# Row maxima in two groups per projection task of a transformer block, and more of them in pairs

## The chip, the cores and the metric

The kernel runs on one core of a Trainium2 chip. It uses that core's engines: TensorE (PE, with PEld for its weight loads), VectorE (DVE), ScalarE (ACT), GpSimd (POOL) and SyncE (SP), which here issues most of the DMAs. The metric is device time of one execution in microseconds (us), as the median of several runs. One further execution is profiled; its span, from the first to the last instruction, is the time base of every trace quoted here. The granted TensorE clock was 1.000 over the whole profiled span.

## The reference

One transformer block with adaptive layer norms, in fp32, on 2048 tokens of width 448:

```python
mod = (silu(c) @ w_mod).reshape(1, 6, 1, -1)      # sa, ca, ga, sb, cb, gb
h = layernorm(x) * (1 + ca) + sa
qkv = h @ wqkv                                     # 16 heads of 28
scores = einsum("bhqd,bhkd->bhqk", q, k) * 28**-0.5
o = einsum("bhqk,bhkd->bhqd", softmax(scores), v)
x = x + ga * (o @ wo)
h = layernorm(x) * (1 + cb) + sb
x = x + gb * (gelu(layernorm(h) @ w1 + b1) @ w2 + b2)   # w1: 448 x 1792
```

The weights are drawn large, so the scores are too, and the softmax needs the maximum of each row of scores before the exponentials.

## The kernel before

Tokens lie in four blocks of 512 and the 16 heads in four groups of four; a head is padded to 32 rows, so the four heads j of a group fill the 128 partitions in quarters. Most matrix products are made from two parts of each number (hi and lo in float32r), so a product over 448 has eleven terms: three row chunks with hi x hi, hi x lo and lo x hi, and two for the last half chunk.

**First phase** (0 to 181 us). After the first norm and the modulation, a loop over blocks b = 0 to 3 runs a list of tasks. A task is one product of eleven matmuls of 512 (or 448) columns into a PSUM tile `pa`: q or k of one head group (`qk_task`), or v of 128 tokens (`v_task`). Block 0 has 14 tasks, blocks 1 and 2 have 12, block 3 has 10, since q and k of head group 0 for the next block stand in the block before. In four tasks of blocks 0, 1 and 2 the next block's normalised tokens are transposed as well; I call them turning tasks.

**The row maxima.** The exact softmax maximum is not needed: the maximum of the hi parts' scores serves. For head group g, query block qt, key block cch, 128 queries i and head j, one matmul with 32 rows and 512 columns (`max_mm`, L392) writes 128 x 512 scores into a PSUM bank `mx` (or `o`), and VectorE reduces them to 128 numbers in `mxp` (`max_one`, L397). There are 4 x 4 x 4 x 16 = 1024 of these. For 48 places of head group 0, key blocks 0 and 1 are taken as a **pair**: one matmul with the difference of the two key tiles, a Relu on ScalarE into a third of `d0` (L405), one matmul with key block 0, and one VectorE operation that adds both and takes the maximum (L409). A pair has two matmuls, as two single maxima have, but one VectorE operation in place of two. When all 64 maxima of a head group and query block are there, `max_fin` reduces them over the key blocks (L429), and the result is written into spare rows of the stored q.

Behind each product of the first phase `emit_task` issues one group of maxima: the first matmuls of its pairs, two singles, the second matmuls of the same pairs, and the other singles. Block 0 has four VectorE operations per task, later blocks up to five; the last task of the phase has none. Five banks `mx`, one `o` and two `pa` are in use. The four quarters of the rows can hold four heads' matmuls side by side.

**Attention** (181 to 846 us). 16 units (head group, query block) of 16 steps. Step: twelve score matmuls in 32 rows (L1046) in two halves, two exponentials on ScalarE (L1051), four matmuls with v for the step before (L1016), and the maxima that the first phase left, in a fixed rhythm of 4 and 3 per step. `n_maxima` puts surplus ones into the steps of the last units that hold the output projection (steps 8 to 11 of units 12 to 15, L317); what is left after the last maximum runs without them. **MLP**: from 846 us on.

[...]

Of the kernel before, what the change touches and what calls it, by code (L numbers as in the profile page):

```python
# [22 lines left out]
D = 448  # L23
# [10 lines left out]
P1RATE = 4  # L34
# [7 lines left out]
def tile_adaln_block(ctx: ExitStack, tc: tile.TileContext, x, wqkv, wo, w1, b1, w2, b2, c, w_mod, out):  # L42
# [272 lines left out]
    def mm_acc(p, terms):  # L315
        for i, (a, b) in enumerate(terms):
            pe.matmul(p, a, b, start=(i == 0), stop=(i == len(terms) - 1))  # L317
# [18 lines left out]
    def qk_task(b, kind, g, done=0, begun=None):  # L336
        p, ts = begun or qk_terms(b, kind, g)
        for i in range(done, len(ts)):
            pe.matmul(p, *ts[i], start=(i == 0), stop=(i == len(ts) - 1))  # L339
# [12 lines left out]
        full = sbt("full", [128, 512], bufs=3)  # L352
        lo = sbt("lo", [128, 512], F32R, bufs=3)
        act.activation(full, p, AF.Identity, bias=bias)

        def split():
            (act.copy if b else dve.tensor_copy)(hi, full)
            if kind == 1 and (g, b) == (0, 1):
                k_diff.append(sbt("raw", [128, 512], F32R, bufs=3))
                pool.tensor_tensor(out=k_diff[0], in0=f(hi), in1=f(kh_sb[(0, 0)]), op=ALU.subtract)  # L360
            pool.tensor_tensor(out=lo, in0=full, in1=f(hi), op=ALU.subtract)
            sl = slice(b * 512, (b + 1) * 512)
            sp.dma_start(f(dscr[kind][0][g])[:, sl], f(hi))
            sp.dma_start(f(dscr[kind][1][g])[:, sl], f(lo))

        return split

    def v_task(b, t):
        p = ps_s()
        ts = slice(t * 128, (t + 1) * 128)  # L370
        hh, hl = hT[b]
        mm_acc(p[:, :D], terms448(
            lambda k: hh(k)[:, ts], lambda k: hl(k)[:, ts], lambda k: wv[0][:, k, :], lambda k: wv[1][:, k, :],
        ))
        emit_task(*p1_n)
        act.copy(v_sb[b][:, t, :, :DH], p[:, :D].rearrange("p (h d) -> p h d", d=DH))
# [6 lines left out]
    k_diff = []  # L383
    paired = ((0, 1), (0, 2), (0, 3))
# [16 lines left out]
    def pair_diff(g, qt, i, j):  # L401
        m = max_mm(g, qt, i, j, k_diff[0])
# [22 lines left out]
    def max_fin(g, qt):  # L425
        m32 = sbt("m32", [128, 32], F32R, bufs=2)
        c0 = 1 if (g, qt) in paired else 0
        pool.memset(f(m32)[:, 16:32], 0.0)
        dve.tensor_reduce(  # L429
            out=m32[:, 0:16].rearrange("p (h i) -> p h i", i=4),  # L430
            in_=mxp[(g, qt)][:, :, :, c0:].rearrange("p i h c -> p h i c"), op=ALU.max, axis=AX.X, negate=True,
        )
# [20 lines left out]
    def queue_max(g, qt, cch):  # L453
# [4 lines left out]
        if (g, qt) in paired and cch < 2:  # L458
            if cch == 1:
                pxq.extend((g, qt, i, j) for i in range(4) for j in range(4))  # L460
            return
        for i in range(4):
            for j in range(4):
                mxq.append((g, qt, cch, i, j))
# [38 lines left out]
    def emit_task(n, sixth, n_pairs):  # L503
# [3 lines left out]
        rests = [pair_diff(*m) for m in pairs]  # L507
        js = [m[3] for m in pairs]
        n_ops = n - len(pairs) + (sixth and len(pairs) > 0)
        singles = []  # L510
        for x in range(n_ops - len(pairs)):
            if mxq:

                free = [j for j in range(4) if j not in js] or range(4)
                fits = [y for y, m in enumerate(mxq[:16]) if m[:3] == mxq[0][:3] and m[4] == free[x % len(free)]]
                singles.append(mxq.pop(fits[0] if fits else 0))
        ops = [lambda ps, m=m: max_one(*m, ps) for m in singles]
        ops[2:2] = rests
        for x, op in enumerate(ops):
            op(ps_o if x + len(pairs) == 5 else ps_mx)  # L520
        for g, qt, cch, i, j in singles:
            count(g, qt, [cch])
        for g, qt, i, j in pairs:
            count(g, qt, [0, 1])

    p1_n = [0, False, 1]
# [25 lines left out]
    def mod_fin():  # L552
# [5 lines left out]
        for j, name in enumerate(("ga", "sb", "cb", "gb")):  # L558
# [41 lines left out]
    for b in range(NB):  # L600
# [11 lines left out]
        for n, (tb, kind, g) in enumerate(tasks):  # L612
            post = []
            ready, newq = newq, []
            p1_n[0] = P1RATE if b < 1 else P1RATE + 1
            if not more and n == len(tasks) - 1:
                p1_n[0] = 0

            k = n - (5 if b < 2 else 4)
            p1_n[1] = not (more and (0 <= k < NC)) and not (b == 1 and n < 4)  # L620
            p1_n[2] = (3 if n > 4 else 1) if b == 3 else 2 if b == 2 and p1_n[1] else 1
# [8 lines left out]
            else:  # L630
                v_task(tb, g)
            for item in ready:
                queue_max(*item)
# [43 lines left out]
    assert not pxq  # L677
# [23 lines left out]

    wo_p = [slot(f"e{part}", [128, NG, D]) for part in range(2)]
# [451 lines left out]
```

## Time and profile before

| | |
|---|---|
| median of 3 runs | 1149.93 us (1149.39 to 1150.04) |
| profiled execution: span | 1147.0 us |
| what the runs' median has beside that span | 2.93 us |
| TensorE busy | 1134.5 us (99%) |
| VectorE busy | 828.7 us (72%) |
| ScalarE busy | 682.5 us (60%) |
| GpSimd busy | 216.8 us (19%) |
| first score matmul of attention | 181.25 us |

A row of a timeline has the start in us, the duration of all its instructions together, engine, line, operation, tiles and shapes, their count, and in brackets the idle time ahead of it with what ended it. Matmuls are pipelined: their starts say how fast they follow each other, their ends are modelled. A row of groups has the busy sum and the mean duration in ns, then the engine's idle time ahead of these instructions. A row of waits has the engine and line that waited, what for, the sum in us, the number of times, and the longest.

### The profile page before, as it was taken

Reading aid. Unit: us, or ns where it says so; the run is one execution under the profiler, and the core shown is the slowest. Engines: PE = TensorE matmul, PEld = TensorE weight load, DVE = VectorE, ACT = ScalarE, POOL = GpSimd, SP = SyncE. Lnnn points to the kernel's source line nnn. Section 1 sums busy time; section 2 is a strip of 40 time slices with the busy share of each in tenths; the row PEclk is TensorE's granted clock in tenths of the full one; section 3 lists DMA queues with packets and bytes.
Section 4 is the critical chain, followed back from the end, with each engine's and each line's share of the span. In section 5 each row is a group of like instructions: output and inputs, shape, how many; then the busy total and the mean of one; then the engine's idle time right before and its main releaser. Section 6 shows DMA issues by size and latency. Waiting matters only on the chain.

```text
span 1147.0 us, 20808 instructions
## 1 busy us (share of the span) xinstructions
PE 1134.5 (99%) x8380; PEld 679.5 (59%) x8380; DVE 828.7 (72%) x1487; ACT 682.5 (60%) x839; POOL 216.8 (19%) x235
## 2 busy tenths in 40 slices
PE   8999999999999999999999999999999999999998
PEld 6767765444443444444444444545458888888887
DVE  6868788999998899989999977583648853444322
ACT  4656757777777877777877777675862321111110
POOL 2534432210000000000000011204514503123000
PEclk9999999999999999999999999999999999999999
DMA  9642354111132111321110222022213100000000
GB/s 299 204 148 110 107 184 130 44 60 57 45 96 66 57 39 38 94 66 57 59 55 21 83 84 62 24 84 68 68 46 95 42 33 1 1 33 1 33 1 33
DMA packets 51305, 81.09 MB, mean 71 GB/s; under 512 B 12700, under 2 KB 21760, under 8 KB 51208
## 3 DMA queue, kind: packets, MB, share of 16 engines
q1 hardware_dynamic: 50248, 78.73, 21.6%
q8 instruction: 66, 1.08, 0.4%
q0 software_dynamic: 672, 0.56, 0.2%
q10 hardware_dynamic: 288, 0.46, 0.1%
q14 instruction: 31, 0.25, 0.1%
HBM read 53.11 MB, written 26.35 MB: 69 GB/s over the span
## 4 chain that ended last, share of the span: by engine, by line
PE 96%; DVE 1%; ACT 1%; issue 1%; SPq 0%; DMA 0%; DVEq 0%; POOL 0%; POOLq 0%; ACTq 0%
PE s L1046 27%; PE o L1016 22%; PE mx L317 16%; PE pa L339 7%; PE mx L392 6%; PE s L1104 4%; PE s L1105 4%; PE s L1103 4%; PE pa L317 3%; PE pa L276 1%; PE o L240 1%; PE mx L240 1%; ACT slot_c L1051 0%; PE o L547 0%; PE pa L279 0%
## 5 line engine op out<-in xcount | busy, mean ns | idle before, releaser
L397 DVE TENSOR_REDUCE mxp<-mx 128x1 f32<-128x512 f32 x919 | 579.6, 685 | 105.9 <-PE mx L392 101.2
L1046 PE MATMUL s<-slot_b,slot_a 32*128 32x512 f32 x3072 | 383.7, 422 | 1.9 <-ACT full L814 0.7
L1051 ACT ACTIVATE slot_c<-s 128x1024 f32<-128x1024 f32 x342 | 331.6, 1022 | 83.8 <-PE s L1046 82.3
L1046 PEld LDWEIGHTS s<-slot_b,slot_a 32*128 32x128 f32 x3072 | 214.4, 183 | 254.5 <-ACT slot_c L1051 151.3
L392 PE MATMUL mx<-kh,qh 32*128 32x512 f32 x899 | 289.6, 470 | 1.2 <-DVE mxp L397 0.9
L1051 ACT ACTIVATE slot_d<-s 128x1024 f32<-128x1024 f32 x170 | 164.8, 1021 | 42.7 <-PE s L1046 42.6
L1016 PE MATMUL o<-slot_c,v 128*32 128x512 f32 x1368 | 183.1, 605 | 0.6 <-ACT osb L984 0.4
L1087 ACT ACTIVATE full<-mx,b_col 128x512 f32<-128x512 f32 x56 | 38.6, 689 | 191.8 <-PE mx L317 175.3
L392 PEld LDWEIGHTS mx<-kh,qh 32*128 32x128 f32 x899 | 116.1, 182 | 8.5 <-DVE mxp L397 5.2
L1090 DVE CAST hi<-full 128x512 fp32r<-128x512 f32 x56 | 25.2, 451 | 129.2 <-ACT full L1087 129.2
L783 POOL TENSOR_TENSOR osb<-osb,osb 128x512 f32<-128x512 f32 x16 | 20.9, 1305 | 463.4 <-DMA osb<-drec 295.1
L1016 PE MATMUL o<-slot_d,v 128*32 128x512 f32 x680 | 90.6, 605 | 0.0
L1016 PEld LDWEIGHTS o<-slot_c,v 128*32 128x32 f32 x1368 | 27.1, 108 | 57.5 <-issue 53.7
L317 PE MATMUL mx<-y,slot_a 128*128 128x512 f32 x160 | 60.6, 395 | 0.0
L405 ACT ACTIVATE slot_d<-mx 128x512 f32<-128x512 f32 x48 | 27.0, 596 | 40.1 <-PE mx L392 40.0
L1091 DVE TENSOR_TENSOR lo<-full,hi 128x512 fp32r<-128x512 f32 x56 | 44.1, 788 | 5.2
L317 PE MATMUL mx<-y,slot_c 128*128 128x512 f32 x152 | 47.5, 396 | 0.1
L1105 PE MATMUL s<-slot_v,lo 128*128 128x448 f32 x128 | 46.7, 365 | 0.0
L1103 PE MATMUL s<-slot_v,hi 128*128 128x448 f32 x128 | 46.6, 364 | 0.0
L317 PE MATMUL mx<-y,slot_v 128*128 128x512 f32 x112 | 39.2, 396 | 0.0
L317 PE MATMUL mx<-y,slot_b 128*128 128x512 f32 x112 | 39.1, 398 | 0.0
L339 PE MATMUL pa<-slot_c,slot_a 128*128 128x512 f32 x136 | 37.0, 405 | 0.0
(223 smaller groups left out, 1388.7 us busy)
## 6 DMA issues: line engine op xcount, KB each, us to landing
d<-lo SPq DMA_DIRECT2D x32, 256.0 KB
slot_b<-d SPq DMA_DIRECT2D x32, 256.0 KB
slot_a<-d SPq DMA_DIRECT2D x32, 256.0 KB
d<-hi SPq DMA_DIRECT2D x20, 256.0 KB
osb<-drec SPq DMA_DIRECT2D x14, 256.0 KB
out_dram<-xn SPq DMA_DIRECT2D x16, 224.0 KB
slot_v<-in_w_mod_dram SPq DMA_DIRECT2D x4, 784.0 KB
raw<-in_B_w_dram SPq DMA_DIRECT2D x14, 224.0 KB
```

Of the source, the lines that this page charges most:

```text
L317: pe.matmul(p, a, b, start=(i == 0), stop=(i == len(terms) - 1))
L339: pe.matmul(p, *ts[i], start=(i == 0), stop=(i == len(ts) - 1))
L392: pe.matmul(m, qh_sb[(g, qt)][js, i * 128 : (i + 1) * 128], k[js, :], start=True, stop=True)
L397: dve.tensor_reduce(out=mxp[(g, qt)][:, i, j, cch : cch + 1], in_=m, op=ALU.max, axis=AX.X)
L1016: pe.matmul(o[32 * j : 32 * j + 32, :], v_sb[kt // 4][:, kt % 4, 4 * g + j, :], p[:, j, :], start=(kt == 0), stop=(kt == NKT - 1),)
L1046: pe.matmul(s2[:, jj, :], ks[rows_, kp, kc], qs[rows_, qp, :], start=(term == 0), stop=(term == 2))
L1051: act.activation(pt[:, 2 * hf : 2 * hf + 2, :], s2, AF.Exp, scale=SCALE)
L1087: act.activation(gf, p, AF.Gelu_apprx_tanh, bias=b1_col[:, i : i + 1])
L1091: dve.tensor_tensor(out=glo, in0=gf, in1=f(ghi), op=ALU.subtract)
L1103: pe.matmul(pp, ghi[:, ts], w_hi, start=(m == 0), stop=False)
L1104: pe.matmul(pp, ghi[:, ts], w_lo, start=False, stop=False)
L1105: pe.matmul(pp, glo[:, ts], w_hi, start=False, stop=(m == NFT - 1))
```

## The change

1. **Two groups per task.** `mm_acc`, which issues a product's terms, can call a function ahead of its seventh term. From block 1 on `burst_mid` stands there: one single maximum and the second matmuls of the pairs begun behind the task before. Behind the product `burst_end` issues four maxima: the first matmuls of up to two pairs, and singles. A turning task begins one pair, others two; block 0 begins none before its last task.
2. **Which heads.** `pick` looks for heads that the group doesn't have yet.
3. **More pairs.** 56 places in place of 48: eight of head group 1, with a second difference tile (`make_diff`, made on GpSimd in block 1). `max_fin` reduces such a mixed query block in two pieces.
4. **Rows.** The second difference tile takes the place that held the broadcast rows sb and cb; these are now loaded when attention begins.

```diff
+    def mm_acc(p, terms, done=0, mid=None):
+        for i in range(done, len(terms)):
+            if i == 6 and mid:
+                mid()
+            pe.matmul(p, *terms[i], start=(i == 0), stop=(i == len(terms) - 1))
...
     def qk_task(b, kind, g, done=0, begun=None):
         p, ts = begun or qk_terms(b, kind, g)
-        for i in range(done, len(ts)):
-            pe.matmul(p, *ts[i], start=(i == 0), stop=(i == len(ts) - 1))
-        emit_task(*p1_n)
+        mm_acc(p, ts, done, burst_mid)
+        burst_end()
...
-    paired = ((0, 1), (0, 2), (0, 3))
+    paired = {(0, qt, i) for qt in range(1, 4) for i in range(4)} | {(1, 1, 0), (1, 1, 1)}
+
+    def make_diff(g, t):
+        k_diff[g] = t
+        pool.tensor_tensor(out=t, in0=f(kh_sb[(g, 1)]), in1=f(kh_sb[(g, 0)]), op=ALU.subtract)
...
-    def emit_task(n, sixth, n_pairs):
+    def pick(js):
+        for j in js:
+            fits = [y for y, m in enumerate(mxq[:16]) if m[:3] == mxq[0][:3] and m[4] == j]
+            if fits:
+                return mxq.pop(fits[0])
+        return mxq.pop(0)
+
+    rests = []
+
+    def singles(n, js, sixth):
+        picked = []
+        for _ in range(n):
+            if mxq:
+                picked.append(pick(js))
+                js = [j for j in js if j != picked[-1][4]]
+        for x, m in enumerate(picked):
+            max_one(*m, ps_o if sixth and x == n - 1 else ps_mx)
+        for g, qt, cch, i, j in picked:
+            count(g, qt, [cch])
+
+    def burst_end():
+        n, sixth, n_pairs, _ = p1_n
         if not n:
             return
         pairs = [pxq.pop(0) for _ in range(min(n_pairs, len(pxq)))]
...
+        rests.extend((m, pair_diff(*m)) for m in pairs)
+        used = [m[3] for m in pairs]
+        singles(n - len(pairs), [j for j in range(4) if j not in used], sixth)
+
+    def burst_mid():
+        now = rests[:]
+        rests.clear()
+        used = [m[3] for m, _ in now]
+        singles(p1_n[3], [j for j in range(4) if j not in used], False)
+        for m, rest in now:
+            rest(ps_mx)
+        for (g, qt, i, j), _ in now:
             count(g, qt, [0, 1])
...
-            p1_n[0] = P1RATE if b < 1 else P1RATE + 1
-            if not more and n == len(tasks) - 1:
-                p1_n[0] = 0
...
+            turning = more and 0 <= k < NC
+            last = not more and n == len(tasks) - 1
+            sixth = not turning and not (b == 1 and n < 4)
+            p1_n[:] = [0 if last else 4, sixth, 0 if b == 0 and n < 13 else 1 if turning else 2, 0 if b == 0 else 1]
```

What stands where now. On TensorE, between two products at the start of block 3, the order was this (`pa` is a product, `raw` the difference tile, `kh_69` key block 0, `kh_417` key block 3, `qh_407` query block 3, `qh_54` query block 0):

```order
L339 MATMUL pa_1805<-slot_c_355_1490,slot_a2h_128 128x512
L392 MATMUL mx_1818<-raw_725,qh_407_1718 128x512
L392 MATMUL mx_1821<-kh_417_1756,qh_54_329 128x512
L392 MATMUL mx_1824<-kh_417_1756,qh_54_329 128x512
L392 MATMUL mx_1827<-kh_69_382,qh_407_1718 128x512
L392 MATMUL mx_1830<-kh_417_1756,qh_54_329 128x512
L392 MATMUL o_1833<-kh_417_1756,qh_54_329 128x512
L339 MATMUL pa_1844<-slot_c_355_1490,slot_a_13_125 128x512
```

Six maxima stood in one group between two products, both matmuls of a pair among them. The same place with the change (L318 is the product's line now, L396 the maxima's; `kh_443` is key block 3, `qh_432` query block 3):

```order
L318 MATMUL pa_1920<-slot_c_375_1551,slot_a_14_126 128x512
L396 MATMUL mx_1927<-kh_443_1835,qh_54_329 128x512
L396 MATMUL mx_1930<-kh_69_382,qh_432_1794 128x512
L396 MATMUL mx_1933<-kh_69_382,qh_432_1794 128x512
L318 MATMUL pa_1920<-slot_c_376_1552,slot_a_13_125 128x512 x3
L318 MATMUL pa_1920<-slot_c_375_1551,slot_a_14_126 128x512
L318 MATMUL pa_1920<-slot_c_375_1551,slot_a_13_125 128x512
L396 MATMUL mx_1941<-raw_725,qh_432_1794 128x512
L396 MATMUL mx_1944<-raw_725,qh_432_1794 128x512
L396 MATMUL mx_1947<-kh_443_1835,qh_54_329 128x512
L396 MATMUL o_1950<-kh_443_1835,qh_54_329 128x512
L318 MATMUL pa_1961<-slot_c_375_1551,slot_a_15_127 128x512
```

Three maxima now stand inside the product, between its sixth and seventh term, and four behind it; the pair's second matmuls are a product away from its first. Over the whole phase there are 258 of these matmuls in place of 222, and 202 VectorE operations on them in place of 174.

In attention, step 201, one of those with an output projection, was this on TensorE:

```order
L317 MATMUL mx_8957<-slot_e_514_2139,lo_8903 128x448
L1046 MATMUL s_8971<-slot_b_1820_8144,slot_a_1900_8518 128x512 x2
L392 MATMUL mx_8974<-kh_1601_7130,qh_1533_6820 128x512
L1046 MATMUL s_8971<-slot_b_1820_8144,slot_a_1900_8518 128x512 x2
L392 MATMUL mx_8979<-kh_1601_7130,qh_1533_6820 128x512
L1046 MATMUL s_8971<-slot_b_1820_8144,slot_a_1900_8518 128x512 x2
L1046 MATMUL s_8985<-slot_b_1820_8144,slot_a_1900_8518 128x512 x2
L392 MATMUL mx_8988<-kh_1601_7130,qh_1533_6820 128x512
L1046 MATMUL s_8985<-slot_b_1820_8144,slot_a_1900_8518 128x512 x4
L1016 MATMUL o_8689<-slot_d_1993_8936,v_257 32x512 x4
```

and is this with the change:

```order
L318 MATMUL mx_9068<-slot_e_550_2248,lo_9013 128x448
L1071 MATMUL s_9082<-slot_b_1856_8254,slot_a_1938_8632 128x512 x6
L1071 MATMUL s_9090<-slot_b_1856_8254,slot_a_1938_8632 128x512 x6
L1041 MATMUL o_8799<-slot_d_2030_9047,v_257 32x512 x4
L318 MATMUL mx_9102<-slot_e_550_2248,slot_a2h_8841 128x448
```

The three maxima of that step are gone. In the whole of attention there are 766 in place of 802: the steps with output projections lose all their 18 (three each in 201 to 203, seven in 217 to 219, two in 233), and the rhythm of 4 and 3 ends after step 226, where it ended after step 231 (18 fewer).

More of the change, by code (lines that the diff above doesn't have):

```diff
@@ L426, in max_fin @@
         m32 = sbt("m32", [128, 32], F32R, bufs=2)
-        c0 = 1 if (g, qt) in paired else 0
         pool.memset(f(m32)[:, 16:32], 0.0)
[L429 to L432, printed above, removed]
+        c0 = [int((g, qt, i) in paired) for i in range(4)]
+        for i0, i1 in [(0, 4)] if len(set(c0)) == 1 else [(0, 2), (2, 4)]:
+            dve.tensor_reduce(
+                out=m32[:, 0:16].rearrange("p (h i) -> p h i", i=4)[:, :, i0:i1],
+                in_=mxp[(g, qt)][:, i0:i1, :, c0[i0] :].rearrange("p i h c -> p h i c"),
+                op=ALU.max, axis=AX.X, negate=True,
+            )
         def put():
@@ L457, in queue_max @@
         left.setdefault((g, qt), 64)
[L458 to L461, printed above, removed]
         for i in range(4):
             for j in range(4):
-                mxq.append((g, qt, cch, i, j))
+                if cch > 1 or (g, qt, i) not in paired:
+                    mxq.append((g, qt, cch, i, j))
+                elif cch == 1:
+                    pxq.append((g, qt, i, j))
         mxq.sort(key=lambda m: (m[:2] != (0, 0), -m[0] if phase1[0] else m[0], m[1:]))
@@ L506, in emit_task @@
         pairs = [pxq.pop(0) for _ in range(min(n_pairs, len(pxq)))]
[L507 to L523, printed above, removed]
+        rests.extend((m, pair_diff(*m)) for m in pairs)
[9 more added lines that the diff above has]
+        for (g, qt, i, j), _ in now:
             count(g, qt, [0, 1])
-    p1_n = [0, False, 1]
+    p1_n = [0, False, 0, 0]
     def finish_max(g, qt):
@@ L631, in tile_adaln_block @@
                 v_task(tb, g)
+            if (b, n) == (1, 4):
+                make_diff(1, sbt("row2", [128, 512], F32R))
             for item in ready:
@@ L676, in tile_adaln_block @@
             stages = later
-    assert not pxq
+    assert not pxq and not rests
     finish_max(0, 0)
@@ L700, in tile_adaln_block @@
                 queue_max(g, qt, cch)
+    row2 = sbt("row2", [128, 2, D])
+    for j, name in ((1, "sb"), (2, "cb")):
+        rows[name] = row2[:, j - 1, :]
+        sp.dma_start(rows[name], drow[j][None].broadcast_to([128, D]))
     wo_p = [slot(f"e{part}", [128, NG, D]) for part in range(2)]
```

19 lines of the change are left out of this document (6 added, 13 removed).

## The prediction

> **What bounds the kernel now.** I read the stages first, then the order of time on TensorE inside the first phase, then the waits. The table by stage (time, then busy time and instructions of PE, PEld, DVE, ACT and POOL, granted clock, DMA share, GB/s) has the span cut where the maxima begin, where block 1 begins, where attention begins, where the output projections of the last head group begin, and where the MLP begins:
>
> ```profile
> span 1147.0 us, 20808 instructions
> core 0: us, PE busy (x) PEld busy (x) DVE busy (x) ACT busy (x) POOL busy (x), PEclk, DMA share, GB/s
> 31.80:60.50 28.70, 28.70 (x148) 21.25 (x147) 26.73 (x50) 16.01 (x27) 16.57 (x16) 1.00 0.62 202
> 60.50:181.20 120.70, 120.12 (x629) 83.10 (x628) 91.75 (x202) 78.76 (x142) 42.01 (x43) 1.00 0.43 144
> 181.20:681.30 500.10, 498.21 (x4706) 219.09 (x4706) 449.78 (x754) 394.78 (x413) 42.48 (x48) 1.00 0.20 62
> ```
>
> The change works in the second stage, 60.5 to 181.2 us. TensorE is busy there for 120.12 of 120.70 us; VectorE, which reduces the maxima, for 91.75, that is 76%. So VectorE has some 29 us of room and TensorE none. Busy TensorE says little by itself, so I looked at what its time is made of. First tasks with four maxima behind them (block 0), then one with six (block 3):
>
> ```profile
> 49.17 0.51 PE L392 MATMUL mx<-raw,osb 32*128 32x512 f32 x4
> 49.61 2.79 PE L339 MATMUL pa<-slot_c,slot_a 128*128 128x512 f32 x11
> 52.33 0.51 PE L392 MATMUL mx<-raw,osb 32*128 32x512 f32 x4
> ...
> 54.03 0.39 PE L339 MATMUL pa<-slot_c,slot_a3h 128*128 128x512 f32 x1
> 54.26 0.62 PE L339 MATMUL pa<-slot_c,slot_a 128*128 128x512 f32 x2
> ```
>
> ```profile
> 140.51 0.49 PE L392 MATMUL mx<-raw,qh 32*128 32x512 f32 x2
> 140.52 0.50 PE L392 MATMUL mx<-raw,osb 32*128 32x512 f32 x2
> 140.85 0.39 PE L392 MATMUL mx<-kh,qh 32*128 32x512 f32 x1
> 140.85 0.39 PE L392 MATMUL o<-kh,qh 32*128 32x512 f32 x1
> 141.17 2.78 PE L339 MATMUL pa<-slot_c,slot_a 128*128 128x512 f32 x11
> 143.88 0.50 PE L392 MATMUL mx<-raw,qh 32*128 32x512 f32 x2
> ```
>
> Starts are what counts. Products follow each other by 0.23 us (54.03 to 54.26), so eleven alone are 11 x 0.23 = 2.53 us. A task with one group of four, from group to group, takes 52.33 - 49.17 = 3.16 us: the group costs 0.63 us. Of this 0.44 lies from its start to the next product (49.17 to 49.61); the other 0.19 are the last product before it and the first behind it, which each take about 0.1 longer than their neighbours. The four maxima start at once because their heads lie in different quarters of the rows. With six, two must reuse a quarter: they start 0.34 us later (140.51, 140.85), as a second round. That task takes 143.88 - 140.51 = 3.37 us, so its group costs 0.84. **A group costs 0.63 us, and each round behind the first 0.21.** How many maxima are in a round hardly matters.
>
> What a maximum costs later, in attention, is seen where there are steps with and without:
>
> ```profile
> 684.30 0.50 PE L1046 MATMUL s<-slot_b,slot_a 32*128 32x512 f32 x2
> 684.31 0.50 PE L392 MATMUL mx<-kh,qh 32*128 32x512 f32 x2
> 684.64 0.85 PE L1046 MATMUL s<-slot_b,slot_a 32*128 32x512 f32 x8
> 685.11 0.39 PE L392 MATMUL mx<-kh,qh 32*128 32x512 f32 x1
> 685.33 0.40 PE L1046 MATMUL s<-slot_b,slot_a 32*128 32x512 f32 x2
> 685.66 1.06 PE L1016 MATMUL o<-slot_d,v 128*32 128x512 f32 x8
> ...
> 792.27 0.98 PE L1046 MATMUL s<-slot_b,slot_a 32*128 32x512 f32 x12 [0.68 <-ACT full L814]
> 793.18 1.07 PE L1016 MATMUL o<-slot_c,v 128*32 128x512 f32 x8
> ...
> 798.73 1.14 PE L1046 MATMUL s<-slot_b,slot_a 32*128 32x512 f32 x12
> ...
> 802.71 1.20 PE L1046 MATMUL s<-slot_b,slot_a 32*128 32x512 f32 x12
> 462.20:501.80 39.60, 31.01 (x33) 1.00 0.28 82
> ...
> L1051 ACT ACTIVATE slot_c<-s 128x1024 f32<-128x1024 f32 x342 | 331.6, 1022 | 83.8 <-PE s L1046 82.3
> ```
>
> In a step with an output projection the twelve score products take 0.91 us without maxima (792.27 to 793.18) and 1.36 with three (684.30 to 685.66): 0.15 us for each. Plain steps: the row of 39.60 us counts the exponentials (L1051, two a step) over one whole unit of 16 steps, with seven maxima in every two steps: 39.60 / 16 = 2.475 us. Two steps without take 802.71 - 798.73 = 3.98, 1.99 each. (2.475 - 1.99) / 3.5 = 0.14 us for each.
>
> **The change part by part.** The order of the built programs gives the counts; times are from the rows above.
>
> *Groups inside the products.* In blocks 1 to 3 (12 + 12 + 10 tasks) every product is cut after six of its eleven terms, and one to three maxima stand there: 34 new groups. Each leaves the eleven products for narrow matmuls and comes back, just as a group behind does: 34 x 0.63 = +21.4 us. What could hide it is TensorE's idle time, and there is none (120.12 of 120.70).
>
> *Groups behind.* 34 groups from the last v task of block 0 on had a repeated quarter each, so two rounds. In the new order they have four maxima; going through the heads, 27 of them have four different quarters, 7 repeat one: -27 x 0.21 = -5.7. Of the new groups inside, two repeat a quarter: +0.4.
>
> *Stalls.* Some groups now wait for a bank that VectorE has not read yet:
>
> ```profile
> PEld mx L392 <- DVE mxp L397: 2.7, 8, 0.4
> L397 DVE TENSOR_REDUCE mxp<-mx 128x1 f32<-128x512 f32 x87 | 56.8, 685 | 25.8 <-PE mx L392 25.8
> L409 DVE CUSTOM_DVE_ANT_0 slot_d<-mx,slot_d 128x512 f32<-128x512 f32 x37 | 25.0, 683 | 4.3 <-ACT slot_d L405 4.3
> L405 ACT ACTIVATE slot_d<-mx 128x512 f32<-128x512 f32 x48 | 27.0, 596 | 40.1 <-PE mx L392 40.0
> ```
>
> The first row holds 22 to 182 us: 2.7 us in eight times. I let half of it go, -1.4, since the second half of a pair now comes a product later, when its Relu is done (ends: 0 and -2.7). On VectorE a full task gets five operations, three maxima and two pair sums, 5 x 0.685 = 3.43 us against a TensorE task of 2.53 + 2 x 0.63 = 3.79; a v task is shorter, some 3.5. Queued behind a late reduction are the next reductions, then the narrow matmuls that want their bank, and with them the product. The 28 more operations make 91.75 + 28 x 0.685 = 110.9 us in a stage of about 135, 82%. So TensorE waits little; I add 0.3 (ends 0 and 3: four tasks of block 1 also carry a norm's statistics on VectorE). The eight more Relus are 8 x 0.596 = 4.8 us on ACT, which has 42 us of room. The second difference tile is one more GpSimd subtraction, beside 42.01 us of 120.70 busy: nothing on the path.
>
> *End of the phase.* The last task had eleven products behind its last maxima; now it has five, about 1.2 us, and three reductions of 0.685 follow the group, before attention may have these banks: +0.3 (ends 0 and 1.2).
>
> So the first phase grows by 21.4 - 5.7 + 0.4 - 1.4 + 0.3 + 0.3 = **+15.3 us**.
>
> *Attention.* It inherits 1024 - 258 = 766 maxima where it had 1024 - 222 = 802. The 36 fall out late: 18 in steps with an output projection, which then have none, 18 in the plain steps 226 to 231. 18 x 0.15 + 18 x 0.14 = **-5.2 us**. Ends: -3.8, if ScalarE's two exponentials of 1.02 us a step hold the plain steps back, and -5.9, if the stall of 0.68 in the row at 792.27 goes too.
>
> *Rows and their loads.* Two row broadcasts move from block 1 to the start of attention, on SP's queue behind the reloads of q and k and ahead of the loads of the output weights; they are first used by the second norm, in the last unit. Nothing (ends -1 and +1, for what the later loads meet in the queue).
>
> Sum: 15.3 - 5.2 = +10.1 on the profiled 1147.0, or 1157.1. The runs' median 1149.93 is 2.93 above that span; with the same rest 1160.0.
>
> [...]
>
> **The rivals.**
>
> *Weights come early (faster).* TensorE could load the narrow weights while products still run, and a cut inside a product might then cost only its round. For it: the program has no wait there. 34 x 0.21 = 7.1 in place of 21.4 makes the sum -4.2: 1145.7. It decides from the point at which a cut costs less than 0.33 us ((21.4 - 10.1) / 34). Against it: the groups behind have no wait either, and their first load starts with their first matmul, after an idle stretch:
>
> ```profile
> 101.75 0.18 PEld L392 LDWEIGHTS mx<-raw,qh 32*128 32x128 f32 x1 [0.36 <-issue]
> 101.76 0.49 PE L392 MATMUL mx<-raw,qh 32*128 32x512 f32 x1
> 102.47 0.19 PEld L339 LDWEIGHTS pa<-slot_b,slot_a 128*128 128x128 f32 x1 [0.24 <-issue]
> ```
>
> [...] The 0.36 us of idle loading in the first row speak against it here.
>
> *VectorE becomes the bound (slower still).* Five operations, 3.43 us and two accumulator reads, against 3.5 in a v task: with the statistics of block 1 on top it may fall behind, with only five banks between, and the backlog carries into attention. Price: 3 us in the first phase and 1.2 at its end in place of 0.6, some 1163.6. Against: 82% over the stage.
>
> *Nearly no change.* The edges of a cut (0.19) hide, all 2.7 us of stalls go, nothing is added to them, and attention gives 5.9: 15.3 - 34 x 0.19 - 1.3 - 0.6 - 5.9 = +1.0, or 1150.9. For it: behind a cut the same tile goes on accumulating, where behind a group a new one begins. Against: the edges are seen at each group of the rows above.
>
> **How the numbers follow.** Forecast 0.76, VectorE 0.10, nearly no change 0.07, early weights 0.07. The time is the forecast's, 1160.0. The range: my own ends add up to 1156.4 and 1167.4; since the other cases hold more below than above, it goes down to 1152, beside nearly no change (that rival and early weights are left out), and up to 1165 (VectorE's rival and the upper ends of attention and stalls). A measurement of this kernel tells 0.2%, 2.3 us, from no change: faster 0.08, same 0.07, slower 0.85.
>
> **What would show it.** In the new profile attention's first scores should start near 196 us in place of 181.25. From group to group the tasks of block 3 should take about 3.8 us in place of 3.4, and a product's sixth and seventh terms should stand about 0.85 us apart. VectorE's share in the stage should be near 82%, its waits for TensorE still its largest. Steps 200 to 203 should take about 0.45 less each where they lost three maxima, and the MLP should be unchanged. I am wrong if the cut product takes under 2.9 us with its group, if TensorE waits for VectorE by more than 3 us in the stage, or if attention is shorter by 10 us.

## The result

The changed kernel takes **1163.82 us** in the median (1161.67 to 1164.97, 4 runs) where the kernel before, beside it on the same chip, takes 1149.66 (1148.94 to 1150.04): ratio **1.0111 [1.0088, 1.0134]**, slower by 14.2 us. The forecast was 1160.0 us, slower than before. The profiled spans say the same: 1161.8 and 1147.0, 14.8 more. The forecast for the span was +10.1, so 4.7 us of the 14.8 are still to be found.

The table by stage of the changed kernel, cut at the same places of the program as in the prediction (columns as there); the two rows of the second block are the kernel before, from the output projections of the last head group to the MLP, and the MLP:

```profile
61.43:197.20 135.77, 135.11 (x665) 82.93 (x664) 110.14 (x238) 82.67 (x150) 43.20 (x45) 1.00 0.39 129
197.20:698.00 500.80, 497.96 (x4688) 218.47 (x4692) 447.45 (x753) 392.53 (x411) 40.51 (x46) 1.00 0.20 62
698.00:860.80 162.80, 160.48 (x1350) 81.76 (x1346) 71.48 (x128) 116.57 (x131) 46.09 (x43) 1.00 0.18 56
860.80:1161.80 301.00, 295.65 (x1400) 250.66 (x1398) 148.34 (x272) 62.88 (x101) 62.17 (x51) 1.00 0.09 29
```

```profile
681.30:846.50 165.20, 163.77 (x1376) 84.58 (x1374) 93.79 (x161) 114.93 (x130) 43.91 (x41) 1.00 0.18 55
846.50:1147.00 300.50, 295.13 (x1394) 250.42 (x1388) 147.91 (x272) 62.38 (x100) 62.19 (x51) 1.00 0.09 29
```

Blocks 1 to 3 grew from 120.70 to 135.77, +15.07. Attention's long part went from 500.10 to 500.80, its end from 165.20 to 162.80, so attention gave 1.7 in all. Block 1 begins 0.93 later, and the MLP takes 0.5 more. Of the 0.93, 0.73 are there already at the first maxima (32.55 us for 31.82), and over the profiles of the experiments that leave block 0 as it is, block 1 begins anywhere from 60.3 to 61.4 us; so this part is not shown to come from the change. 0.93 + 15.07 - 1.7 + 0.5 = 14.8. The stage of the change did what was forecast (+15.3); attention did not (-5.2).

What a cut looks like is seen in the timeline of the changed kernel on TensorE, one task at the start of block 2:

```profile
112.57 0.49 PE L396 MATMUL mx<-row,osb 32*128 32x512 f32 x2
...
113.00 1.67 PE L318 MATMUL pa<-slot_b,slot_a 128*128 128x512 f32 x6
114.60 0.50 PE L396 MATMUL mx<-raw,osb 32*128 32x512 f32 x3
115.03 0.73 PE L318 MATMUL pa<-slot_b,slot_a 128*128 128x512 f32 x2
...
116.39 0.50 PE L396 MATMUL mx<-row,osb 32*128 32x512 f32 x2
```

From group to group (112.57 to 116.39) the task takes 3.82 us. The group behind takes 0.43 (112.57 to 113.00), the group inside also 0.43 (114.60 to 115.03), although one has four maxima and the other three. The eleven terms take 1.60 + 1.36 = 2.96. All 22 q and k products of the stage were like this, 1.59 and 1.36 in the mean, where the kernel before took 2.74 for the eleven in one piece; of the 12 v products, the eleven that another task follows took 1.40 + 1.22 for 2.42. **So a cut costs 0.43 to 0.45 us for the group and 0.20 to 0.21 for the two new edges**, 0.65 together: 34 x 0.65 = +22.2. The groups behind fell from 0.70 in the mean (20 of six, 0.73; 14 of five, 0.66), 23.8 us in all, to 0.50 and 16.9 us: -7.0. 22.2 - 7.0 = +15.2, which is the stage.

### The profile page after: what moved, and what is told of

Read it like the earlier page. It is cut to its first block, busy times and chain, and to the rows that moved or that the text cites. A ratio compares the mean times of both kernels' runs of the same rounds, so it can differ in the third digit from the quotient of the medians.

```text
span 1161.8 us, 20810 instructions
## 1 busy us (share of the span) xinstructions
PE 1145.3 (99%) x8380; PEld 674.5 (58%) x8380; DVE 822.9 (71%) x1488; ACT 686.4 (59%) x847; POOL 218.2 (19%) x236
## 3 DMA queue, kind: packets, MB, share of 16 engines
q1 hardware_dynamic: 50248, 78.73, 21.4%
## 5 line engine op out<-in xcount | busy, mean ns | idle before, releaser
L401 DVE TENSOR_REDUCE mxp<-mx 128x1 f32<-128x512 f32 x886 | 560.1, 684 | 106.5 <-PE mx L396 98.6
L1071 PEld LDWEIGHTS s<-slot_b,slot_a 32*128 32x128 f32 x3072 | 212.0, 183 | 253.6 <-ACT slot_c L1076 147.3
L396 PE MATMUL mx<-kh,qh 32*128 32x512 f32 x894 | 289.1, 476 | 2.4 <-DVE mxp L401 2.0
L396 PEld LDWEIGHTS mx<-kh,qh 32*128 32x128 f32 x894 | 114.2, 182 | 19.7 <-DVE mxp L401 12.2
L318 PE MATMUL mx<-y,slot_a 128*128 128x512 f32 x160 | 60.6, 395 | 0.0
L409 ACT ACTIVATE slot_d<-mx 128x512 f32<-128x512 f32 x56 | 30.8, 596 | 48.3 <-PE mx L396 30.3
L318 PE MATMUL mx<-y,slot_c 128*128 128x512 f32 x152 | 47.5, 396 | 0.1
L318 PE MATMUL pa<-slot_c,slot_a 128*128 128x512 f32 x136 | 39.6, 417 | 0.0
L318 PE MATMUL mx<-y,slot_v 128*128 128x512 f32 x112 | 39.2, 396 | 0.0
L318 PE MATMUL mx<-y,slot_b 128*128 128x512 f32 x112 | 39.0, 398 | 0.0
```

Source lines behind the costliest of these rows:

```text
L318: pe.matmul(p, *terms[i], start=(i == 0), stop=(i == len(terms) - 1))
L396: pe.matmul(m, qh_sb[(g, qt)][js, i * 128 : (i + 1) * 128], k[js, :], start=True, stop=True)
L401: dve.tensor_reduce(out=mxp[(g, qt)][:, i, j, cch : cch + 1], in_=m, op=ALU.max, axis=AX.X)
L409: act.activation(r, m, AF.Relu)
L1071: pe.matmul(s2[:, jj, :], ks[rows_, kp, kc], qs[rows_, qp, :], start=(term == 0), stop=(term == 2))
```

## The experiments

In all of them the kernel before was run beside, with medians of 1150.9 to 1151.8 us; ratios are to it. The time of a unit runs from the first exponential of its 16 steps to the first of the next unit (of unit 15, to that of its last step), in the profile of each kernel.

**Cuts without more maxima.** In the changed kernel the single maximum inside each product is left where it was queued, so only the second matmuls of pairs stand inside: 32 cuts, and 224 maxima ahead of attention (before 222, changed 258).

```
-  p1_n[:] = [0 if last else 4, sixth, 0 if b == 0 and n < 13 else 1 if turning else 2, 0 if b == 0 else 1]
+  p1_n[:] = [0 if last else 4, sixth, 0 if b == 0 and n < 13 else 1 if turning else 2, 0]
```

> The changed kernel without the single maximum inside the products: only the second matmuls of the pairs stand there, so 32 of the 34 cuts stay, with 224 maxima in the first phase in place of 258. If the cuts are what the change costs, the first scores come only about 1.7 us earlier than with the change (two cuts fewer, two rounds fewer), near 195.6 us, and attention gets 34 maxima back, 34 x 0.145 = 5 us: 1167 us. If the cost lies in the number of maxima or in VectorE's 34 operations, the first phase shrinks by 34 x 0.44 = 15 us to about 182, and the time is near 1154.

Measured: 1166.34 us, 1.0133 [1.0117, 1.0148]. With nearly as many maxima ahead of attention as before, the kernel is as slow as the changed one: it is the cuts, not the number of maxima or VectorE's work. By the prices above 32 cuts are +20.8, and the groups behind, now 0.44 in the mean for 0.70, 34 x 0.26 = -8.8. Attention's first exponential comes 15.0 us later than in the kernel before: 12.0 by these prices, and 3.5 by an idle of 4.1 us at the phase's end (0.6 before), which the next experiment has too. The first scores start at 195.62 us, as expected, but in part by luck: the idle was not in that working, and block 1 began 1.1 us earlier than in the changed kernel.

**The same maxima, no cut.** As the last, but the second matmuls stand at the end of the group behind the product:

```
-  mm_acc(p, ts, done, burst_mid)
+  mm_acc(p, ts, done)
   ...
   singles(n - len(pairs), [j for j in range(4) if j not in used], sixth)
+  burst_mid()
```

> The same 224 maxima as in the run with pairs' seconds alone inside the products, in the same order, but the seconds stand at the end of the group behind the product that began the pair: no product is cut. If a cut costs 0.63 us and a second round 0.21, this is 32 x 0.42 = 13.4 us shorter than that run, less up to 3 us for banks that are not free yet: first scores between 182 and 185.5 us, 1153.5 to 1157. If where the maxima stand does not matter, both runs are equal.

Measured: 1156.84 us, 1.0048 [1.0033, 1.0063], 9.5 us less than with the cuts. It is still 5.7 above the kernel before. The profile shows two places. Four groups of block 1 take 1.60 us where the others of six take 0.66, since their last matmul waits until ScalarE has read one of the five banks; the sixth is taken there. That is 3.8 us. And at the end of the phase the first unit's maxima are done only with the last group. The timeline there, with the queue of SyncE (SPq), then the table by stretches (the granted clock is the third number from the end):

```profile
182.02 0.22 DVE L434 TENSOR_REDUCE m<-mxp 128x16 fp32r<-128x64 f32 x1
...
183.60 2.33 SPq L445 DMA_DIRECT2D slot_b<-full  x4
...
187.34 0.79 PE L1072 MATMUL s<-slot_b,slot_a 32*128 32x512 f32 x2 [4.10 <-DMA slot_b<-full]
```

```profile
183.20:186.20 3.00, 0.05 (x1) 0.00 (x0) 0.38 (x3) 0.53 (x1) 0.00 (x0) 1.00 0.03 7
186.30:187.30 1.00, 0.00 (x0) 0.00 (x0) 0.00 (x0) 0.00 (x0) 0.00 (x0) 0.50 0.12 29
188.00:192.00 4.00, 3.62 (x29) 2.58 (x23) 3.46 (x6) 2.10 (x3) 0.00 (x0) 0.50 0.90 212
192.00:196.00 4.00, 4.00 (x28) 1.40 (x23) 1.57 (x4) 1.77 (x2) 0.64 (x1) 0.50 0.52 163
```

The first scores need the maxima as rows of slot_b. The last of them leave VectorE behind the reduction at 182.02, four transfers bring them, and TensorE idles for 4.10 us. Its granted clock is 0.50 from 186.3 to 196.4 us, and the first unit takes 41.79 us for the 39.80 of before. The run with cuts has the same idle (4.14 us), 0.50 for as long, and 41.72. The clock is at 0.50 some 3.0 us behind the end of the last product, which is modelled (183.24), and further below it falls with far less idle time (none over 0.62 us); so that the idle brought it down is not shown.

**Part of the maxima left out of the kernel before**, which measures what one costs in attention.

```
+  if (g, qt) == (3, 3) and cch in (1, 3):
+      return
   ...
```

This kernel leaves out half of that unit's maxima and raises the remaining ones by 300 in their place (the lines behind the dots).

> The kernel before with 32 maxima fewer in attention (head group 3, query block 3, key blocks 1 and 3 are left out of the row maximum, which is raised by 300 in their place); 32 of the 36 places that the change empties in attention are emptied, and the first phase and all that happens in attention before step 201 stay as they were. If a maximum costs 0.14 to 0.15 us there, 4.6 us less: 1145. If attention as a whole only gives the 1.7 us that the changed kernel's trace shows between the same two marks, since ScalarE or transfers hold the steps, 1148.

Measured: 1148.1 us, 0.9975 [0.996, 0.999], some 3 us less. On ScalarE, the starts of the exponentials of two steps in a row, both with output projections; first this kernel, then the kernel before, then the changed kernel:

```profile
685.09 1.94 ACT L1057 ACTIVATE slot_c<-s 128x1024 f32<-128x1024 f32 x2 [0.43 <-PE s L1052]
689.03 1.94 ACT L1057 ACTIVATE slot_c<-s 128x1024 f32<-128x1024 f32 x2 [0.42 <-PE s L1052]
```

```profile
685.37 1.94 ACT L1051 ACTIVATE slot_c<-s 128x1024 f32<-128x1024 f32 x2 [0.43 <-PE s L1046]
689.75 1.94 ACT L1051 ACTIVATE slot_c<-s 128x1024 f32<-128x1024 f32 x2 [0.43 <-PE s L1046]
```

```profile
704.48 1.94 ACT L1076 ACTIVATE slot_c<-s 128x1024 f32<-128x1024 f32 x2 [0.43 <-PE s L1071]
708.42 1.94 ACT L1076 ACTIVATE slot_c<-s 128x1024 f32<-128x1024 f32 x2 [0.43 <-PE s L1071]
```

A step with three maxima takes 4.38 us (685.37 to 689.75), without them 3.94 in both other kernels: 0.44 / 3 = 0.147 each. Units 12 to 14 together take 145.2 us before, 140.5 here (32 maxima less, -4.7) and 140.3 in the changed kernel (36 less, -4.9). The price of a maximum in attention was right in these units. The whole run gave less than the 4.6 expected: its profiled span is 4.0 shorter, since unit 15 took 44.40 for 43.39. What the changed kernel gains in units 12 to 14 it loses elsewhere.

**Where attention loses it.** Unit 4 took 41.42 us before and takes 43.54 in the changed kernel, unit 8 39.96 and 41.07, unit 15 43.39 and 44.01. The timeline of the changed kernel in unit 4 (SyncE's queue, VectorE, ScalarE):

```profile
356.75 0.90 SPq L591 DMA_DIRECT2D slot_b<-d  x2
...
362.49 2.28 SPq L445 DMA_DIRECT2D slot_b<-full  x4
...
364.87 0.57 SPq L793 DMA_DIRECT2D den<-osb  x1
366.82 0.25 DVE L799 RECIPROCAL den<-den 128x16 f32<-128x16 f32 x1 [3.00 <-DMA den<-osb]
...
368.89 1.94 ACT L1076 ACTIVATE slot_d<-s 128x1024 f32<-128x1024 f32 x2 [2.40 <-PE s L1071]
```

The same place in the kernel before:

```profile
348.81 0.58 SPq L768 DMA_DIRECT2D den<-osb  x1
350.71 0.25 DVE L774 RECIPROCAL den<-den 128x16 f32<-128x16 f32 x1 [2.39 <-DMA den<-osb]
...
352.79 1.94 ACT L1051 ACTIVATE slot_d<-s 128x1024 f32<-128x1024 f32 x2 [1.77 <-PE s L1046]
```

The four transfers at 362.49 put the maxima into the next unit's slot_b, so they wait until its load from 356.75 has landed (4.8 us of wait on this queue). The denominators' small transfer stands behind them, VectorE's next instruction is their reciprocal, and VectorE stands still for 3.00 us, with all reductions behind it. TensorE gets no bank, ScalarE no scores. Before, the wait was 2.39. In the changed kernel the four transfers leave 5.74 us after the load was issued (356.75 to 362.49), before 5.02 us (341.41 to 346.43).

That is not all of unit 4's loss of 2.12 us. The step with the stall takes 4.33 us for 3.71, 0.6 more; the next one takes 4.59 for 3.06, 1.5 more. In that one the granted clock is at a half, while the kernel before has 1.00 there:

```profile
366.00:369.00 3.00, 1.45 (x13) 0.62 (x13) 2.18 (x5) 0.60 (x2) 0.00 (x0) 1.00 0.06 5
370.00:373.40 3.40, 3.40 (x23) 1.27 (x21) 1.99 (x5) 0.83 (x1) 0.00 (x0) 0.50 0.47 150
```

TensorE had worked for 1.45 of the 3 us from 366. Whether the stall brought the clock down is not shown: the kernel before has the stall without the fall. In unit 8 VectorE waits 2.03 us at the same reciprocal, 0.71 before.

The test takes these small transfers off that queue, to GpSimd's, in the changed kernel (the same line stands at both places that issue them):

```
-  q_ = pool if u >= NU - 2 else sp
+  q_ = pool
```

> The changed kernel with the three small transfers at the end of each unit (denominators out and back, reciprocals) issued on GpSimd's queue in all units, not on SP's. If the long steps 66, 67, 130, 131 and 184 come from VectorE waiting for a transfer that stands behind others on SP's queue, they go: 4.0 + 1.5 + 0.6 = some 6 us less than the change, 1158. If the transfers are late because the DMA engines are full, nothing changes: 1163 to 1164.

Measured: 1160.36 us, 1.0079 [1.0064, 1.0094], and a profiled span of 1157.4 for 1161.8: 4.4 less. Unit 4 is down to 40.94, unit 8 to 39.68, unit 11 to 39.70 from 40.21, unit 15 to 43.04; unit 2 got a stall of its own (41.02 for 39.67). In units 4 and 8 VectorE no longer waits at the reciprocal, and the granted clock is 1.00 throughout: there the order of that queue was behind the loss, with the half clock in unit 4 beside it. Unit 11 has no wait at the reciprocal in either kernel; VectorE waits there for GpSimd, whose multiplication needs the last of the three transfers (0.73 us in the changed kernel, 0.24 in this run). Unit 15 is another matter: its transfers stand on GpSimd's queue without the edit too, and its ninth step takes from 4.55 to 6.00 us in the profiles of this case (4.97 before, 5.61 changed). Of the 4.4 us, 1.0 came in that unit and 0.6 ahead of block 1; neither is the edit's. The same edit in the kernel before:

> The kernel before, with the three small transfers of each attention unit's denominators on GpSimd's queue instead of SyncE's, in all units (before, only the last two units have them there). Theory 'order of SyncE's queue': the kernel before has the same stalls at the ends of units as the changed one, only smaller (steps 66 and 67 take 3.71 and 3.06 us for a normal 2.20 and 2.75, that is 1.8 us; step 132 and 184 some 0.4 us each; step 248 another 1 to 2 us), since these small transfers stand behind four that wait; without them the run takes 2 to 3 us less than before, 1147 to 1148 us. Rival 'the bytes set it': the stalls move to other steps and the run is within 0.5 us of before.

Measured: 1151.92 us, 1.0009 [0.9997, 1.002]. This falls for the theory as put: unit 4 did lose its stall (41.42 to 39.72), but units 2, 5, 8 and 12 to 15 each lost 0.2 to 0.7 us, 3.4 together. In units 12 to 14 VectorE now waits at the reciprocal, for 0.79, 1.12 and 1.32 us, where it did not wait before; so there GpSimd's queue is the slower way. In units 2, 5 and 8 it does not wait there, and unit 15 was not moved; their losses stay unexplained. If moving pays only where SyncE's queue stalls, it should pay when that one unit alone is moved:

```
-  q_ = pool if u >= NU - 2 else sp
+  q_ = pool if u == 3 or u >= NU - 2 else sp
```

> The kernel before with the small transfers of the denominators on GpSimd's queue for one more unit, the fourth, whose end stalls for 1.8 us on SyncE's queue. Theory 'the stall is that queue's order at that place, and the other places lost by the longer way over GpSimd's queue': 1.7 us less than before, ratio 0.998 to 0.999. Rival 'what is taken from one unit comes back in another': ratio 0.9995 to 1.001.

Measured: **1148.52 us, 0.9977 [0.9964, 0.999]**, a little faster than both kernels. A part of this is the granted clock: among the runs with a mean clock of 0.999 or 1.000 the medians are 1148.4 us and 1149.7 for the kernel before (seven runs each), and the profiled spans, both at 1.000, are 1146.5 and 1147.0. Its timeline in unit 4:

```profile
344.44 0.91 POOL L768 DMA_DIRECT2D den<-osb  x1 [23.52 <-ACT osb L984]
...
346.80 2.28 SPq L439 DMA_DIRECT2D slot_b<-full  x4
...
348.58 0.24 DVE L774 RECIPROCAL den<-den 128x16 f32<-128x16 f32 x1
```

The denominators leave ahead of the four transfers, and VectorE no longer waits at the reciprocal (no bracket). Unit 4 takes 39.94, 1.5 less. In this profile unit 8 took 40.91 for 39.96, with 1.62 us of wait at its reciprocal for 0.71, so 0.9 of it came back there, as the rival said; the ratio's interval still lies below 1.

**More cuts.** The group inside each product of the changed kernel is split in two: its single ahead of the fourth term, the pairs' second matmuls ahead of the seventh.

```
-  if i == 6 and mid:
-      mid()
+  if i in (3, 6) and mid:
+      mid(i)
```

> The changed kernel with the group inside each product split in two: its single maximum ahead of the fourth term, the second matmuls of the pairs where they were, ahead of the seventh. The same maxima, the same products, 34 more cuts. Theory 'the price is of the cut': each new cut costs the 0.42 us by which the experiment without cuts was cheaper, up to the 0.63 us of the forecast, so 14 to 21 us more: 1178 to 1185 us. Rival 'the price is of the 32-row matmuls in it': the same matmuls in two places cost what they cost in one, 1163 to 1165 us.

Measured: 1179.13 us, 1.0249 [1.0234, 1.0263], 15.3 us above the changed kernel; attention starts 18.1 us later. (Counted in the program, it has 32 new cuts, not 34, since two groups inside held only the single.) TensorE's timeline, a product of block 2:

```profile
141.72 0.95 PE L318 MATMUL pa<-slot_b,slot_a 128*128 128x512 f32 x3
142.59 0.50 PE L396 MATMUL mx<-kh,qh 32*128 32x512 f32 x1
143.02 0.50 PE L318 MATMUL pa<-slot_b,slot_a 128*128 128x512 f32 x1
...
143.93 0.50 PE L396 MATMUL mx<-kh,qh 32*128 32x512 f32 x1
144.35 0.73 PE L318 MATMUL pa<-slot_b,slot_a 128*128 128x512 f32 x2
```

One maximum alone takes 0.43 us from its start to the next term (142.59 to 143.02), the same as three or four. The price is the cut's. 18.1 / 32 = 0.57 us each in the whole. (Attention itself took 2.1 us less in this profile, so the span grew by 16.0.)

**All in one group.** 257 of the 258 maxima of the changed kernel behind the products, up to seven in a row:

```
-  mm_acc(p, ts, done, burst_mid)
+  mm_acc(p, ts, done)
   ...
   singles(n - len(pairs), [j for j in range(4) if j not in used], sixth)
+  burst_mid()
```

> The changed kernel with all its maxima kept (258 ahead of the first scores), but in one group behind each product: up to seven in a row, none inside. Theory 'a cut costs 0.63, but behind the product there are banks for six only': the cuts give 34 x 0.63 = 21 us back, the longer groups cost 34 x 0.21 = 7, and the seventh waits 0.4 to 0.9 us for VectorE to free a bank, 14 to 29 us: 1163 to 1178 us, so no gain by putting them together. Rival 'the banks are no limit': 1149 to 1151 us.

Measured: 1179.2 us, 1.025 [1.0229, 1.0271]. Its waits between 60 and 200 us, then a group of seven on TensorE:

```profile
PEld mx L396 <- ACT slot_d L409: 25.3, 32, 0.9
```

```profile
178.50 0.50 PE L396 MATMUL mx<-raw,qh 32*128 32x512 f32 x2
...
178.84 0.45 PE L396 MATMUL mx<-kh,qh 32*128 32x512 f32 x2
179.69 0.50 PE L396 MATMUL mx<-kh,qh 32*128 32x512 f32 x1 [0.40 <-ACT slot_d L409]
180.11 1.20 PE L318 MATMUL pa<-slot_c,slot_a 128*128 128x512 f32 x4
```

The seventh has no bank. It starts 0.85 us behind the sixth, and the group takes 1.61 us (178.50 to 180.11) where one of six takes 0.66. The bank it waits for is that of a pair's first matmul, so ScalarE's Relu gives it back, not VectorE as I had expected. The sum lies just above the upper end that I had given. So with these six banks, six is the limit behind a product; more need a cut or another bank.

**Does the spread of the pairs cost?** No cuts (the edit of the last experiment stays), the pairs on the change's 56 places, and as many per task as before (one, two, or three in the last block), with the first unit's maxima done four tasks ahead of the end. The edit also lets block 0 take five or six maxima behind a task, where it took four:

```
-  p1_n[:] = [0 if last else 4, sixth, 0 if b == 0 and n < 13 else 1 if turning else 2, 0]
+  n_pairs = 0 if b == 0 and n < 13 else 1 if turning or (b == 1 and n < 4) else 2
+  if b == 3 and n:
+      n_pairs = 3 if n > 4 else 1
+  p1_n[:] = [0 if last else 6 - (0 if sixth else 1) - n_pairs, sixth, n_pairs, 0]
```

> The pairs over both halves of the first head group and into the second as in the change, no cuts, and the number of pairs per task as before (one where five banks are free, two where six are, one and then three in the last block), so that no group has over six maxima, and the first unit's maxima are done four tasks ahead of the end: 224 maxima ahead of the first scores, 222 before. Theory 'the cuts alone made the change slow': without them, without waits for a bank and without a late first unit nothing is left of the 7 us that the experiment with six behind the product still cost: 1149 to 1152 us. Rival 'the spread of the pairs costs by itself' (24 more Relu reads on ScalarE, two more k differences on GpSimd, the two half transposes of the row maxima): 1155 to 1157 us.

Measured: 1154.08 us, 1.0026 [1.0011, 1.004], between the two. In its last block the four tasks with three pairs stand 4.0 us apart. TensorE, one of their groups:

```profile
181.48 0.39 PE L396 MATMUL mx<-kh,qh 32*128 32x512 f32 x2
182.33 0.49 PE L396 MATMUL mx<-kh,qh 32*128 32x512 f32 x1 [0.46 <-ACT slot_d L409]
```

The last of the six waits again for ScalarE to free one of the five banks, while the sixth bank stands empty: only single maxima used it. So it was tried once more with that bank:

```
-  for m, rest in now:
-      rest(ps_mx)
+  for x, (m, rest) in enumerate(now):
+      rest(ps_o if p1_n[1] and x == 2 else ps_mx)
```

> The spread without cuts again, with one thing mended: in the last block's four tasks with three pairs and no single maximum, the third second matmul takes the sixth bank, where it waited 0.45 us for ScalarE to read one of the five (those tasks were 4.0 us apart, 3.1 to 3.4 in the kernel before). Theory 'the spread of the pairs costs nothing by itself': the four tasks come back to about 3.2 us (3 us less), and with the shorter idle at the phase's end TensorE's granted clock stays at 1.00 where it fell to 0.52 for some 6 us (1 to 2 us less): 1149 to 1151 us, within 0.2% of the kernel before. Rival 'the spread costs': 1152 to 1155 us.

Measured: 1150.12 us, 0.9992 [0.9982, 1.0002]: no cost of the spread is left that this could tell. The first experiment had as many maxima in this phase and 32 cuts; it lies 1.4% above this run, 16 us, with its idle of 4.1 us among them. The same group, and the stretches of 4 us at the phase's end:

```profile
176.30 0.40 PE L396 MATMUL mx<-kh,qh 32*128 32x512 f32 x2
176.31 0.39 PE L396 MATMUL o<-kh,qh 32*128 32x512 f32 x1
176.63 2.50 PE L318 MATMUL pa<-slot_e,slot_c 128*128 128x448 f32 x11
```

```profile
184.00:188.00 4.00, 3.57 (x23) 1.79 (x24) 3.85 (x7) 3.26 (x4) 0.00 (x0) 0.69 0.99 311
188.00:192.00 4.00, 4.00 (x28) 1.67 (x24) 1.68 (x3) 1.58 (x2) 1.91 (x3) 0.50 0.23 61
192.00:196.00 4.00, 4.00 (x39) 1.40 (x31) 3.05 (x6) 2.97 (x4) 1.17 (x2) 0.95 0.22 59
```

The four tasks are back to 3.1 to 3.3 us. The clock, which I had expected to stay at 1.00, fell to 0.50 all the same in the profiled execution, with no idle of TensorE over 0.62 us ahead of it.

## Why the prediction was right, and where it missed

*Cuts, 34 x 0.63 = +21.4, and +0.4 for two that repeat a quarter.* Right. Measured 0.65 each, those two included, +22.2. The sixth and the seventh term stand 0.76 us apart, not 0.85: 0.1 of the edges lies behind the seventh. The rival "weights come early" (0.21 a cut) falls, and so does "nearly no change" (0.44): each new cut cost 0.57 in the whole, and the kernel with as many maxima and no cut (six banks) is 16 us shorter than the one with 32 cuts, though its groups behind are longer. Groups of one, three and four maxima all took 0.43 us between full-height products (142.59 to 143.02 in the run with two cuts, 114.60 to 115.03 and 112.57 to 113.00 in the changed kernel).

*Groups behind, -5.7; stalls, -1.4 and +0.3.* The sum of -6.8 came out as -7.0. How it divides between rounds and stalls the trace does not tell: 27 groups of one round and 7 of two, at 0.44 and 0.66, would be 16.5 us, and the 34 took 16.9.

*VectorE.* 110.14 us busy in the stage, 81%, for the forecast 110.9 and 82%. But I had written that I'd be wrong if TensorE waited for VectorE by more than 3 us. The waits of the changed kernel in the stage:

```profile
PEld mx L396 <- issue: 15.2, 45, 0.4
PEld pa L318 <- issue: 14.3, 56, 0.4
PEld mx L396 <- DVE mxp L401: 6.2, 18, 0.4
```

It waited 6.2, in 18 pieces of at most 0.4. That sign was badly chosen. The weight load of a group stands idle for up to 0.4 us at the edge anyway (the first row, "issue"), so a bank that comes free in that time need delay nothing (for TensorE's matmuls themselves the profile lists no wait in the stage); the 0.4 us between 16.5 and 16.9 are what the 18 waits can have cost in the groups behind. VectorE did not become the bound.

*End of the phase, +0.3.* Right within the trace: the first scores wait 0.82 us for ScalarE's copy of v, 0.62 before. With the 0.93 ahead of block 1, which no term held and most of which is there before the first maxima, the first scores start at 197.35, not 196.

*Attention, -5.2.* **This is the step that missed.** Its working was right, 0.147 a maximum and -4.9 in units 12 to 14, but the total was -1.7. I had written under "Rows and their loads" that the later loads may meet something in the queue, with ±1 us. In fact units 4, 8, 11 and 15 took 4.4 us more than before: 2.1, 1.1, 0.6 and 0.6. In units 4 and 8 the traces show VectorE waiting for the denominators, which SyncE's queue holds behind four transfers that wait; in unit 4 that is 0.6 of the 2.1, and 1.5 fall in the step at half clock. Unit 11 has a smaller wait for the same chain, and unit 15's loss has another cause, which stays open. The kernel before already had 1.8 us of the stall in unit 4, in rows that the prediction does not show. Why the stalls became longer in the changed kernel was not tried; the row broadcasts that the change moved and the shifted moment of the loads are both possible.

*The span and the run.* I took 2.93 us beside the span; the profiled run had 1.8 (1163.58 for 1161.8). *MLP*: 0.5 more, forecast unchanged; the cause is open.

So the direction and its cause were right, the first phase to 0.2 us. The 3.8 us that the median lies above the forecast are 3.5 in attention (stalls of transfers, and one step at half clock), 0.9 ahead of block 1, 0.5 in the MLP and 0.2 by which the median lies above the profiled run, less 0.2 in the first phase and 1.1 in what lies beside the span. In the stage of the change the working held; that the 2.93 us beside the span were 1.1 too many hid a part of what attention missed, and that is luck.

## What to carry to other kernels

In this kernel a change from full-height to 32-row matmuls and back has a price per visit, 0.65 us with up to one maximum per row quarter (0.57 for each new cut in the run with two). Measure that price in yours, make the visits few and fill them up to the free banks, and count the banks before adding one more: here a group of six took 0.66 us, and one of seven, without a bank for the last, 1.61. When work is moved out of a stage, price what the shift does to the DMA queue there as well: look for transfers that wait in a queue, as the four here did for 4.8 us, and for what small transfer stands behind them. Move such a transfer to another queue only at the place where the profile shows the stall, and expect little: here that gained 0.1 to 0.2%, and moving it everywhere gained nothing.

## What was unexpected of the hardware

One narrow matmul, three, and four in four row quarters took the same 0.43 us between full-height products, in the run with two cuts and in the changed kernel.

In eight of the twelve profiled executions the mean granted clock was under 1.000 (0.994 to 0.999). Inside at least seven of them it fell to 0.50 for about 3.4 us at a time (the changed kernel, 370.0 to 373.4), 6.8 (the spread pairs with six banks, at the start of attention) or 10.2 (the same maxima without a cut, 186.3 to 196.4): mostly at the start of attention, in unit 4 in three of them, and in the first phase in two. It fell behind an idle of 4.1 us, but also with no idle of TensorE over 0.62 us (six banks) or, in the run with two cuts, where the mean was 0.998, over 0.43 us in the 10 us ahead of it. What sets it off is open, and whether it falls differs between runs of one kernel (the kernel before: means from 0.995 to 1.000). Among the 23 runs of the kernel before in the last comparison six had a mean granted clock of 1.000 over the execution, with a median of 1149.7 us, and six of 0.995 or 0.996, all between 1152.7 and 1154.2; where in the execution it fell in these is not recorded. At 1.000 the kernel with spread pairs and six banks has 1149.6, in the median of four. Most of the 5 us between the lowest and the highest run of this kernel goes with it.
